# First batch in text order with a fence behind it, and weight maxima spread by TensorE, in a filter-and-experts kernel

## The chip, the cores and the metric

The kernel runs on one core of one Trainium2 chip. The metric is the device time of one execution in microseconds (us), the median over several runs. Engines are named as in the profile: PE is TensorE's matmul side (PEld its weight load), DVE is VectorE, ACT is ScalarE, POOL is GpSimd, SP is SyncE, which here only issues DMAs.

## What is computed

```python
def _attn_ref(x, filt_r, filt_i):            # x: 8 x 2496 x 256
    X = np.fft.rfft(x, axis=1)
    Y = X * (filt_r + 1j * filt_i)[None, :, :]
    return np.fft.irfft(Y, n=x.shape[1], axis=1)

def _moe_ref(x, expert_emb, tau, w1, w2):    # x: 19968 x 256, 8 experts, F = 1024
    xn = x / (norm(x) + 1e-06); en = expert_emb / (norm(expert_emb) + 1e-06)
    logits = xn @ en.T / tau
    expert_idx = np.argmax(logits, axis=1)
    gate_w = softmax(logits)[arange(N), expert_idx]
    for e in range(8):
        mask = expert_idx == e
        out[mask] = gate_w[mask, None] * (np.maximum(x[mask] @ w1[e], 0.0) @ w2[e])
```

A filter along the sequence, then each row goes to the expert with the largest cosine and comes back weighted.

## The kernel before

The eight batches go one after the other through four stages. **S1** (`conv_s1`): 11 tiles of x, each a product with the constant c1 (L403), a copy on ACT (L426) and a write to SD in DRAM. **S2** (`conv_s2`): ten tiles `a` read back from SD; product with c2, copies `xs` that swap the two halves on ACT (L486, L487), filter multiplications on DVE (`yy` L458, `xs` L460), the sum on POOL (L494; for batch 0 there is none, and the product with m1 is taken over both), product with m1 (L512), copy `z` (L515), write to ZD. **SB** (`conv_sb`, the tile loop): 11 tiles of ZD; product `y` (L403), squares on ACT (L587), a power of two near the norm on DVE (`q` L590, `rr` L592), the row's high half on ACT (L559) and low half on DVE (L562), transposes (L606), their copy `yT` on DVE (L608), logits `lp` (L621). A tile's high and low halves are taken one step later than its product and its transposes two. After every four tiles `route` (from L632) makes norms, the choice of an expert, the rank within it (L682) and indices (L704) in small DVE operations, and POOL scatters the rows to XS, grouped by expert (L711). **Slots**: 256 rows of one expert and batch, read transposed from XS (L834); `up` (product `ph` L865, high half `h` on ACT L871, low half on DVE L872), `down` (`po` L892) and a scatter to the output (L900). Slots of a batch run between the stages of the next one.

Weights arrive in fourteen DMAs of 1 MB issued by ACT (L210), each expert's in the place that the next expert's halves will take. `weight_halves` prepares them: largest absolute value along each partition (DVE, L242, L243), the largest over partitions (POOL's all-reduce, L246), scales (L249 to L257), then halves: ACT L271 or L267 and L268, DVE L272, POOL L269.

Most of the program is ordered by a scheduler. `head()` is the first batch: S1 of batch 0, its S2, its SB with batch 1's S1 woven in. In it the instructions of ACT and PE stand in text order (`manual_schedule`), those of the other engines where the scheduler puts them. Step numbers of `head()` set the weights: `WLOADS` gives the steps at which a load is issued (every fourth from the fourth), and from step 20 on preparation goes at 0.6 parts a step. No slot begins before `head()` has ended.

```python
    with tc.manual_schedule(engines={mybir.EngineType.Activation, mybir.EngineType.PE}):
        for n, _ in enumerate(head()):
            for _ in range(WLOADS.get(n, 0)):
                next(loads, None)
            if n >= PREP_AT:
                owed += PREP_RATE
```

Of the kernel before, what the change touches and what calls it, by code (L numbers as in the profile page):

```python
# [49 lines left out]
DLAG = 2  # L50
MID = 8
WLOADS = {4 + 4 * n: 1 for n in range(14)}
PREP_AT, PREP_RATE = 20, 0.6
# [3 lines left out]
def moe_spectral_kernel(  # L57
# [59 lines left out]
    emb_sb = cw.tile([E, D], F32, tag="hl", bufs=XYB, name="emb_sb")  # L117
    for t, a in ((c1_sb, c1), (c2_sb, c2), (m1_sb, m1), (csb_sb, csb), (sgn_sb, sgn),
                 (lt32, lt), (tau_sb, tau), (emb_sb, emb)):
        nc.scalar.dma_start(t, a)  # L120
# [5 lines left out]
    nc.vector.memset(one16, 1.0)  # L126

# [64 lines left out]


# [5 lines left out]
    wall = const.tile([P, E, 2], F32, tag="wall", name="wall")  # L199
# [35 lines left out]
    def weight_halves():  # L235
# [9 lines left out]
        def spread_max(e, js):  # L245
            nc.gpsimd.partition_all_reduce(wall[:, e, js], wmax[:, e, js], P, bass.bass_isa.ReduceOp.max)  # L246

        def scales(e, js):
            v.tensor_scalar(out=wall[:, e, js], in0=wall[:, e, js], scalar1=2.0 ** -100, scalar2=None, op0=ALU.max)  # L249
            v.tensor_scalar(out=wsc[:, e, js].bitcast(I32), in0=wall[:, e, js].bitcast(I32), scalar1=0x7F800000,  # L250
                            scalar2=0x7F800000, op0=ALU.bitwise_and, op1=ALU.bitwise_xor)
# [30 lines left out]
        for e in range(E - 1):  # L282
            if e + 1 < E - 1:
                yield from maxima(e + 1)
            scales(e, slice(0, 2))
            for j in range(4):
# [3 lines left out]
                yield  # L290
        e = E - 1
# [67 lines left out]
    def load(q, g, pool, tag, t, ap, rows, full):  # L359
        it = pool.tile([P, 2, D], F32, tag=tag, name=f"{tag}{g}_{t}")  # L360
        got = []
        for h, k, m in whole(g, ap, t, rows, full):
            q.dma_start(it[:k, h], m)  # L363
# [45 lines left out]

    def conv_s1(g):  # L410
# [20 lines left out]
    def conv_s2(g):  # L431
# [11 lines left out]
        def load_f(k):  # L443
            fts = []
            for k2 in range(k * 2 // nb, (k + 1) * 2 // nb):
                ft = cf.tile([P, 2, D], F32, tag="f", name=f"f{g}_{k2}")
                nc.sync.dma_start(ft, filt[k2])
                fts.append((k2, ft))
            return fts

# [12 lines left out]
        fin = {k: load_f(k) for k in range(2)}  # L463
# [4 lines left out]
        lag = SAL if g else 1  # L468
# [5 lines left out]
        for k in range(NK + lag):  # L474
            if k + INB - 1 < NK:
                ain[k + INB - 1] = load_a(k + INB - 1)
            if k < NK:
                pt = ps_c.tile([P, 2, D], F32, tag="c", name=f"s2_{g}_{k}")
# [13 lines left out]
                ys[k] = [yy]  # L492
# [5 lines left out]
                if k + 2 < NK:  # L498
                    fin[k + 2] = load_f(k + 2)
            yield W_S2  # L500
            j = k - 1
            if g >= G_SA and 0 <= j < NK:
                (_, a), = split(*asides(f"yp{g}_{j}"), [(both, ys[j][0].rearrange("p j c -> p (j c)"))])
                ys[j] = [a]
            j = k - lag
            if 0 <= j < NK:
                zp = ps_c.tile([P, CW], F32, tag="c", name=f"sa_{g}_{j}")
                for n, t in enumerate(ys[j]):
                    if isinstance(t, tuple):
                        product(zp, cons["m1"], t)  # L510
                    else:
                        nc.tensor.matmul(zp, cons["m1"], t.rearrange("p j c -> p (j c)"), start=(n == 0),  # L512
                                         stop=(n + 1 == len(ys[j])))
                zt = cst.tile([P, CW], F32, tag="st", name=f"z{g}_{j}")
# [4 lines left out]
    def conv_sb(g):  # L519
# [22 lines left out]
        if g == G_SB:  # L542
            cons["csb"] = parts_of(cons["csb"], "csb")
        for s in range(NTL + LPL):
            if s + 3 < NTL:
                vin[s + 3] = load_v(s + 3)
            if g >= G_SB:
                for u in (0, 1) if s == 0 else (s + 1,):
                    if u < NTL:
                        vin[u] = split(*pair(f"vp{g}_{u}"), vin[u])  # L550
            part()

            t = s - 1
            if 0 <= t < NTL:
# [5 lines left out]
                for i in range(2):  # L560
                    u = t % CHUNK * 2 + i
                    nc.vector.scalar_tensor_tensor(out=rows[:, i, D:2 * D], in0=y[:, i], scalar=rr[:, u:u + 1],  # L562
                                                   in1=rows[:, i, 0:D], op0=ALU.mult, op1=ALU.subtract)
            t = s
            if t < NTL:
                c = t // CHUNK
                if t % CHUNK == 0:
# [6 lines left out]
                        "rr": rt.tile([P, NTC], F32, tag="rr", name=f"rr{g}_{t}"),  # L574
                    }
# [9 lines left out]
                for i in range(2):  # L585
# [11 lines left out]
                               pattern=[[S if nb == 2 else TOK, 2]], base=b * S + ag * TOK, channel_multiplier=1)  # L597
            yield W_SB
# [33 lines left out]
    def route(g, out_rows, t0, n, rows, ssq, rr, lp):  # L632
# [15 lines left out]
        ssq, rr = ssq[:, :nt], rr[:, :nt]  # L648
# [456 lines left out]
```

## Time and profile before

| | |
|---|---|
| runs of before, us | 1512.34, 1515.03, 1509.94; median 1512.34 |
| profiled execution, us | 1499.08 (span 1497.2) |
| mean granted TensorE clock | 0.924 |
| busy share of the span | PE 87%, PEld 66%, DVE 58%, ACT 46%, POOL 37% |
| bytes moved by DMA | 229.16 MB, 153 GB/s in the mean |

The profiled execution was 13.3 us shorter than the median of the runs, so the working is made against its own 1499.08 us. Busy shares are means over the whole span; the first 219 us, before the first slot's hidden tile, look different from the rest, and are read by stretch. In the rows, idle time stands in square brackets with what ended it.

### The profile page before, as it was taken

The numbers are of one execution on the slowest core, as the hardware profiler recorded it, in microseconds if no ns is written. First come the engines' busy times: TensorE is split into PE (matmuls) and PEld (weight loads), VectorE is DVE, ScalarE is ACT, GpSimd is POOL, SyncE is SP. The second block draws the span as 40 slices with busy tenths as digits, with TensorE's granted clock in tenths as the row PEclk, the third lists the DMA queues.
The fourth block names the chain that finished last, engine by engine and source line by source line (L and its number), as shares of the span: only waits on it lengthen the run. The fifth ranks groups of instructions, "written<-read, shape, count | busy, mean of one in ns | idle before, by whom it ended". The sixth has DMA issues, their size and how long they took to land.

```text
span 1497.2 us, 31982 instructions
## 1 busy us (share of the span) xinstructions
PE 1301.8 (87%) x10956; PEld 988.2 (66%) x10956; DVE 873.5 (58%) x2841; ACT 693.7 (46%) x1578; POOL 548.7 (37%) x614
## 2 busy tenths in 40 slices
PE   5644557998997998899979988997999789999997
PEld 1212235766765776686658666865787578899997
DVE  2558765563474757575648555664658432266664
ACT  2435554543562665375437634662665122333332
POOL 0021454245524543552445254525433431222222
PEclk7876678999998999999989999999999889999999
DMA  8865375646774775577457746674753222122211
GB/s 273 302 213 200 118 211 158 187 133 189 215 188 130 205 217 156 166 220 183 140 166 201 195 121 185 195 192 124 200 169 92 76 67 54 50 49 48 49 45 40
DMA packets 230494, 229.16 MB, mean 153 GB/s; under 512 B 126089, under 2 KB 172497, under 8 KB 228405
## 3 DMA queue, kind: packets, MB, share of 16 engines
q1 hardware_dynamic: 200908, 151.93, 37.7%
q0 software_dynamic: 26400, 60.07, 12.8%
q10 hardware_dynamic: 3017, 15.02, 3.0%
q8 instruction: 92, 1.51, 0.4%
q14 instruction: 77, 0.63, 0.1%
HBM read 121.61 MB, written 84.84 MB: 138 GB/s over the span
## 4 chain that ended last, share of the span: by engine, by line
PE 61%; issue 15%; POOL 3%; DMA 2%; ACT 1%; DVE 1%; another core or an unknown queue 1%; POOLq 0%; SPq 0%; ACTq 0%; DVEq 0%
PE po L892 22%; PE ph L865 21%; PE y L403 5%; PE s L403 5%; POOL out_dram L900 3%; PE tp L606 2%; PE sa L408 2%; PE s L408 2%; DMA f<-ZD 1%; PE lp L621 1%; PE sa L512 1%; DMA ZD<-z 1%; DVE xs L460 0%; DMA f<-in_filt 0%
## 5 line engine op out<-in xcount | busy, mean ns | idle before, releaser
L892 PE MATMUL po<-W,h 128*128 128x256 f16 (+1 forms) x3864 | 519.8, 279 | 27.9 <-issue 27.5
L892 PEld LDWEIGHTS <-h 128*128 128x128 f16 x3864 | 375.5, 100 | 132.4 <-issue 85.3
L865 PE MATMUL ph<-xT,W 128*128 128x256 f16 x3072 | 414.8, 279 | 30.9 <-issue 18.7
L872 DVE SCALAR_TENSOR_TENSOR h<-ph,h 128x512 f16<-128x512 f32 (+1 forms) x388 | 232.0, 598 | 277.6 <-ACT h L871 240.6
L865 PEld LDWEIGHTS <-W 128*128 128x128 f16 x3072 | 300.1, 100 | 129.0 <-issue 91.4
L871 ACT ACTIVATE h<-ph 128x512 f16<-128x512 f32 (+1 forms) x388 | 203.4, 525 | 378.8 <-PE ph L865 205.4
L900 POOL DMA_INDIRECT out_dram<-o,meta x161 | 171.5, 1065 | 359.0 <-ACT o L899 319.4
L711 POOL DMA_INDIRECT XS<-rows,ixi x176 | 176.6, 1004 | 172.4 <-issue 136.2
L403 PE MATMUL y<-f,csb_sb 120*128 120x512 f32 (+1 forms) x192 | 101.2, 612 | 39.8 <-DVE rows L562 17.7
L494 POOL TENSOR_TENSOR yy<-yy,xs 128x512 f32<-128x512 f32 x70 | 94.3, 1349 | 109.1 <-DVE xs L460 69.5
L363 POOL DMA_DIRECT2D in<-in_x x84 | 66.9, 797 | 154.9 <-PE s L403 113.4
L403 PE MATMUL s<-in,c_sb 117*128 117x512 f32 (+1 forms) x192 | 111.1, 672 | 12.8 <-DMA in<-in_x 8.1
L865 PE MATMUL ph<-xT,wp 128*128 128x128 f16 x1584 | 104.9, 219 | 0.2
L865 PEld LDWEIGHTS <-wp 128*128 128x128 f16 x1584 | 96.7, 98 | 3.2 <-issue 0.7
L587 ACT ACTIVATE rows<-y 128x256 f16<-128x256 f32 x176 | 66.0, 384 | 64.7 <-PE y L403 58.8
L559 ACT ACTIVATE rows<-y,rr 128x256 f16<-128x256 f32 x176 | 73.9, 473 | 46.8 <-DVE rr L592 44.7
L426 ACT COPY s<-s 128x512 f32<-128x512 f32 x88 | 51.5, 586 | 91.4 <-PE s L403 43.5
L458 DVE TENSOR_TENSOR yy<-s,f 128x256 f32<-128x256 f32 x160 | 60.9, 419 | 52.5 <-ACT xs L487 39.4
L562 DVE SCALAR_TENSOR_TENSOR rows<-y,rr,rows 128x256 f16<-128x256 f32 x176 | 77.1, 478 | 22.5 <-ACT rows L559 19.8
L853 DVE COPY wp<-W 128x1024 f16 x132 | 62.1, 471 | 45.3 <-PE ph L865 44.8
L899 ACT ACTIVATE o<-po,meta 128x256 f32<-128x256 f32 x161 | 69.4, 475 | 34.2 <-PE po L892 26.7
L460 DVE SCALAR_TENSOR_TENSOR xs<-xs,sgn_sb,f 128x256 f32<-128x256 f32 x160 | 82.0, 551 | 0.0
(170 smaller groups left out, 1397.0 us busy)
## 6 DMA issues: line engine op xcount, KB each, us to landing
f<-in_filt SPq DMA_DIRECT2D x160, 256.0 KB
a<-SD SPq DMA_DIRECT2D x80, 256.0 KB
ZD<-z SPq DMA_DIRECT2D x80, 256.0 KB
SD<-s SPq DMA_DIRECT2D x80, 240.0 KB
f<-ZD SPq DMA_DIRECT2D x80, 240.0 KB
in<-in_x POOLq DMA_DIRECT2D x70, 234.0 KB
W<-in_w ACTq DMA_DIRECT2D x14, 1024.0 KB
XS<-rows,ixi POOLq DMA_INDIRECT x176
```

Source lines behind the costliest of these rows:

```text
L403: nc.tensor.matmul(out_, c[:a.shape[0]], a, start=True, stop=True)
L460: nc.vector.scalar_tensor_tensor(out=o, in0=i, scalar=sgn_sb[:, k2:k2 + 1], in1=f, op0=ALU.mult, op1=ALU.mult)
L494: nc.gpsimd.tensor_tensor(out=yy, in0=yy, in1=xs, op=ALU.add)
L559: nc.scalar.activation(rows[:, i, 0:D], y[:, i], AF.Copy, scale=rr[:, u:u + 1])
L562: nc.vector.scalar_tensor_tensor(out=rows[:, i, D:2 * D], in0=y[:, i], scalar=rr[:, u:u + 1], in1=rows[:, i, 0:D], op0=ALU.mult, op1=ALU.s ...
L711: i = nc.gpsimd.indirect_dma_start(out=XS, out_offset=bass.IndirectOffsetOnAxis(ap=ix, axis=0), in_=src, in_offset=None)
L865: last["pe"] = nc.tensor.matmul(ph[:, fi, :size], wp[:, k * 2 + wh, fi * P:(fi + 1) * P], xT[:, xh * 2 + k], start=(c == 0), stop=(c == 5))
L871: nc.scalar.activation(h[:, 0, :, :size], ph[:, :, :size], AF.Relu)
L872: hd = nc.vector.scalar_tensor_tensor(out=h[:, 1, :, :size], in0=ph[:, :, :size], scalar=0.0, in1=h[:, 0, :, :size], op0=ALU.max, op1=ALU. ...
L892: nc.tensor.matmul(self.po[:, s], self.hs[fp][:, hh, fi, s * P:(s + 1) * P], self.Wp[:, off + wh * 1024:off + wh * 1024 + D], start=(fp == ...
L899: nc.scalar.activation(o, self.po[:, s], AF.Copy, scale=self.meta[:, s, 1:2])
L900: i = nc.gpsimd.indirect_dma_start(out=out, out_offset=bass.IndirectOffsetOnAxis(ap=self.meta[:, s, 0:1].bitcast(I32), axis=0), in_=o, in_ ...
```

## The change

- DVE and SP stand in text order in `head()` too, and a fence of the scheduler (`no_sync_barrier`) behind it keeps later work from moving ahead of it.
- Constants: c1 and c2 on ACT's queue, the rest on POOL's. The experts' embeddings are prepared after S1 (`experts_ready`).
- Batch 0's x loads are all issued at once; all twenty filter slabs are loaded ahead (`FAHEAD`) into the places of experts 5 to 7 in W, four by SP and sixteen by ACT.
- Batch 0's S1 alternates between the two PSUM tiles of `ps_c` and the two of `ps_y`; its S2 has c2's products in `ps_y` and m1's in `ps_c`. It has the sum on POOL and one m1 product a tile, two steps later, as the other batches.
- In batch 0's SB a step first makes the new tile's product and squares, then the earlier tile's halves. Norms are taken out of `route` (`norms`), after the chunk's last squares.
- x loads of later batches are issued behind POOL's last sum.
- The maximum over partitions comes from two small products (one with an fp32 identity, one with ones) and five DVE operations.
- Weights: `WLOADS` names eight steps: expert 0's two loads in S2, those of experts 1 to 3 in SB; the other six behind the fence. `PREPS` prepares expert 0 alone in `head()`.

```diff
-WLOADS = {4 + 4 * n: 1 for n in range(14)}
-PREP_AT, PREP_RATE = 20, 0.6
+FAHEAD = 10
+WLOADS = (22, 26, 44, 50, 56, 62, 68, 72)
+PREPS = (35, 36, 40, 42, 44, 46)
...
         def spread_max(e, js):
-            nc.gpsimd.partition_all_reduce(wall[:, e, js], wmax[:, e, js], P, bass.bass_isa.ReduceOp.max)
+            n = js.stop - js.start
+            m = wmax[:, e, js]
+            v.tensor_scalar(out=m, in0=m, scalar1=2.0 ** -100, scalar2=None, op0=ALU.max)
+            v.tensor_scalar(out=m.bitcast(I32), in0=m.bitcast(I32), scalar1=0x7F800000, scalar2=None,
+                            op0=ALU.bitwise_and)
+            pm = ps_c.tile([P, 2, P], F32, tag="c", name=f"pm{e}_{js.start}")
+            nc.tensor.matmul(pm[:n, 0], m, ident32, start=True, stop=True)
+            v.tensor_reduce(out=wtop[:n, e:e + 1], in_=pm[:n, 0], axis=AX.X, op=ALU.max)
+            v.tensor_scalar(out=wdg[:n, e, :n], in0=ident32[:n, :n], scalar1=wtop[:n, e:e + 1], scalar2=None,
+                            op0=ALU.mult)
+            nc.tensor.matmul(pm[:, 1, :n], one32[:n], wdg[:n, e, :n], start=True, stop=True)
+            v.tensor_scalar(out=wsc[:, e, js].bitcast(I32), in0=pm[:, 1, :n].bitcast(I32), scalar1=0x7F800000,
+                            scalar2=None, op0=ALU.bitwise_xor)
...
+            (nc.scalar if not g and k > 1 else nc.sync).dma_start(ft, filt[k2])
...
+            alone = g == 0 and t % 2
+            pt = (ps_y if alone else ps_c).tile([P, 2, D], F32, tag="y" if alone else "c", name=f"s1_{g}_{t}")
...
+                pt = (ps_c if g else ps_y).tile([P, 2, D], F32, tag="c" if g else "y", name=f"s2_{g}_{k}")
...
-                if g:
-                    nc.gpsimd.tensor_tensor(out=yy, in0=yy, in1=xs, op=ALU.add)
-                else:
-
-                    ys[k].append(xs)
+                last["sum"] = nc.gpsimd.tensor_tensor(out=yy, in0=yy, in1=xs, op=ALU.add)
...
+            for stage in (quantised, rows_of) if g else (rows_of, quantised):
+                stage(s)
...
-    with tc.manual_schedule(engines={mybir.EngineType.Activation, mybir.EngineType.PE}):
+    engines = {mybir.EngineType.Activation, mybir.EngineType.PE, mybir.EngineType.DVE, mybir.EngineType.SP}
+    with tc.manual_schedule(engines=engines):
         for n, _ in enumerate(head()):
-            for _ in range(WLOADS.get(n, 0)):
+            if n in WLOADS:
                 next(loads, None)
-            if n >= PREP_AT:
-                owed += PREP_RATE
-            while owed >= 1:
-                owed -= 1
+            if n in PREPS:
                 next(prep, None)
+    tc.no_sync_barrier()
```

How this moves instructions is shown at three places. First ScalarE, from the last copies of batch 0's S1 to the first of its S2 (`s` is S1's copy, `xs` the swapped halves of S2, W the weights' place). Before:

```order
L426 COPY s0_7_290<-s1_0_7_288 128x512
L426 COPY s0_8_295<-s1_0_8_293 128x512
L210 DMA W_201<-in_w2 128x2048
L426 COPY s0_9_301<-s1_0_9_299 128x512
L426 COPY s0_10_307<-s1_0_10_304 128x512
L210 DMA W_201<-in_w1 128x2048
L486 COPY xs0_0_330<-s2_0_0_328 64x512
L487 COPY xs0_0_330<-s2_0_0_328 64x512
L486 COPY xs0_1_346<-s2_0_1_344 64x512
L487 COPY xs0_1_346<-s2_0_1_344 64x512
```

After:

```order
L472 COPY s0_8_268<-s1_0_8_266 128x512
L472 COPY s0_9_273<-s1_0_9_271 128x512
L472 COPY s0_10_279<-s1_0_10_276 128x512
L182 ACTIVATE esq_283,ess_284<-emb_sb_124 8x256
L190 CAST ehl_305<-esc_303 8x256
L447 DMA W_170<-in_filt 128x512 x16
L526 COPY xs0_0_344<-s2_0_0_342 64x512
L527 COPY xs0_0_344<-s2_0_0_342 64x512
L526 COPY xs0_1_357<-s2_0_1_355 64x512
L527 COPY xs0_1_357<-s2_0_1_355 64x512
```

The two weight loads are gone from here; the squares of the embeddings and sixteen loads of filter slabs stand ahead of the first `xs`.

Second VectorE in the middle of batch 0's tile loop (`rows` is the row buffer, `y` the inverse product, `q` and `rr` the power of two, `wmx` and `wmax` the weights' maxima, `wsc` their scale). Before:

```order
L242 TENSOR_REDUCE wmx_207<-W_201 128x1
L272 SCALAR_TENSOR_TENSOR W_201<-W_201,wsc_205 128x1024
L242 TENSOR_REDUCE wmx_207<-W_201 128x1
L562 SCALAR_TENSOR_TENSOR rows0_4_728<-y0_4_729,rr0_4_727,rows0_4_728 128x256 x2
L590 TENSOR_SCALAR q0_5_786<-ssq0_4_726 128x2
L272 SCALAR_TENSOR_TENSOR W_201<-W_201,wsc_205 128x1024
L243 TENSOR_REDUCE wmax_203<-wmx_207 128x1
L272 SCALAR_TENSOR_TENSOR W_201<-W_201,wsc_205 128x1024
L592 TENSOR_SCALAR rr0_4_727<-q0_5_786 128x2
L242 TENSOR_REDUCE wmx_207<-W_201 128x1 x2
L249 TENSOR_SCALAR wall_204<-wall_204 128x2
L608 COPY yT0_4_845<-tp0_4_836 128x1024
```

After:

```order
L655 COPY yT0_1_674<-tp0_1_665 128x1024
L621 TENSOR_SCALAR q0_4_695<-ssq0_4_687 128x2
L623 TENSOR_SCALAR rr0_4_688<-q0_4_695 128x2
L589 SCALAR_TENSOR_TENSOR rows0_3_627<-y0_3_628,rr0_0_539,rows0_3_627 128x256 x2
L655 COPY yT0_2_720<-tp0_2_711 128x1024
L621 TENSOR_SCALAR q0_5_737<-ssq0_4_687 128x2
L623 TENSOR_SCALAR rr0_4_688<-q0_5_737 128x2
L589 SCALAR_TENSOR_TENSOR rows0_4_690<-y0_4_691,rr0_4_688,rows0_4_690 128x256 x2
L655 COPY yT0_3_754<-tp0_3_745 128x1024
L621 TENSOR_SCALAR q0_6_778<-ssq0_4_687 128x2
L623 TENSOR_SCALAR rr0_4_688<-q0_6_778 128x2
L589 SCALAR_TENSOR_TENSOR rows0_5_732<-y0_5_733,rr0_4_688,rows0_5_732 128x256 x2
```

The reductions and halves of weights are gone from between a tile's operations, which now follow one another tile by tile.

Third VectorE up to the first hidden tile `h` of the first slot. Before:

```order
L242 TENSOR_REDUCE wmx_207<-W_201 128x1 x2
L458 TENSOR_TENSOR yy1_3_1577<-s2_1_3_1572,f1_6_1506 128x256
L458 TENSOR_TENSOR yy1_3_1577<-s2_1_3_1572,f1_7_1508 128x256
L460 SCALAR_TENSOR_TENSOR xs1_3_1574<-xs1_3_1574,sgn_sb_121,f1_6_1506 128x256
L243 TENSOR_REDUCE wmax_203<-wmx_207 128x1
L460 SCALAR_TENSOR_TENSOR xs1_3_1574<-xs1_3_1574,sgn_sb_121,f1_7_1508 128x256
L242 TENSOR_REDUCE wmx_207<-wraw0_1621 128x1
L242 TENSOR_REDUCE wmx_207<-wraw1_1623 128x1
L249 TENSOR_SCALAR wall_204<-wall_204 128x1
L872 SCALAR_TENSOR_TENSOR h0_0_0_1414<-ph0_0_0_1401,h0_0_0_1414 128x512
```

After:

```order
L252 TENSOR_REDUCE wmax_172<-wmx_177 128x1
L272 TENSOR_SCALAR wsc_175<-wsc_175 128x1 x2
L251 TENSOR_REDUCE wmx_177<-W_170 128x1 x2
L274 RECIPROCAL winv_176<-wsc_175 128x2
L291 SCALAR_TENSOR_TENSOR W_170<-W_170,wsc_175 128x1024
L252 TENSOR_REDUCE wmax_172<-wmx_177 128x1
L276 TENSOR_TENSOR isc_171<-winv_176 128x1
L291 SCALAR_TENSOR_TENSOR W_170<-W_170,wsc_175 128x1024
L258 TENSOR_SCALAR wmax_172<-wmax_172 128x2
L251 TENSOR_REDUCE wmx_177<-W_170 128x1 x2
L291 SCALAR_TENSOR_TENSOR W_170<-W_170,wsc_175 128x1024
L923 SCALAR_TENSOR_TENSOR h0_0_0_1275<-ph0_0_0_1262,h0_0_0_1275 128x512
```

Between the last index of batch 0 (L755) and this first `h` (L923) there stand, after the change, 22 of the reductions L251, nine of the halves L291 (experts 1 to 3), 11 of L252, some 44 small operations, and one tile of batch 1's filter; before, most of the weights' operations stood ahead of the last index, and parts of four filter tiles of batch 1 behind it.

## Rows read from the trace of the kernel before

**Rows 1.** Chain that ended last, shares by line (page).
```profile
PE po L892 22%; PE ph L865 21%; PE y L403 5%; PE s L403 5%; POOL out_dram L900 3%; PE tp L606 2%; PE sa L408 2%; PE s L408 2%; DMA f<-ZD 1%; PE lp L621 1%; PE sa L512 1%; DMA ZD<-z 1%; DVE xs L460 0%; DMA f<-in_filt 0%
```

**Rows 2.** By stretch: length, busy PE, PEld, DVE, ACT, POOL, granted clock, DMA share, GB/s.
```profile
4.00:29.00 25.00, 18.81 (x28) 6.37 (x28) 6.14 (x25) 7.73 (x15) 0.00 (x0) 0.80 0.93 288
40.50:93.50 53.00, 35.42 (x60) 12.43 (x60) 33.67 (x70) 22.66 (x35) 7.06 (x7) 0.83 0.81 281
101.80:164.80 63.00, 32.18 (x166) 15.94 (x166) 47.56 (x142) 34.78 (x82) 14.72 (x23) 0.69 0.58 187
164.80:188.80 24.00, 13.75 (x85) 7.92 (x86) 19.67 (x95) 13.37 (x22) 14.80 (x15) 0.57 0.39 116
188.80:219.40 30.60, 13.75 (x41) 6.00 (x40) 18.92 (x33) 13.94 (x19) 19.95 (x17) 0.68 0.77 212
260.00:400.00 140.00, 132.89 (x1043) 96.69 (x1042) 74.08 (x282) 67.45 (x163) 62.27 (x72) 0.98 0.62 181
```

**Rows 3.** TensorE's timeline: start us, us, line, tiles, count, idle before and releaser.
```profile
40.53 3.75 PE L403 MATMUL s<-a,c_sb 128*128 128x512 f32 x4 [11.61 <-DMA a<-SD]
...
101.80 2.08 PE L403 MATMUL y<-f,csb_sb 120*128 120x512 f32 x2 [8.96 <-DMA f<-ZD]
...
126.93 1.13 PE L403 MATMUL y<-f,csb_sb 120*128 120x512 f32 x2
...
137.71 2.08 PE L403 MATMUL y<-f,csb_sb 120*128 120x512 f32 x2 [7.22 <-DVE rows L562]
...
164.76 2.37 PE L403 MATMUL y<-f,csb_sb 120*128 120x256 f32 x4 [6.35 <-DVE rows L562]
...
212.95 2.78 PE L865 MATMUL ph<-xT,W 128*128 128x256 f16 x24 [0.76 <-DMA xT<-XS]
...
219.53 1.47 PE L865 MATMUL ph<-xT,W 128*128 128x256 f16 x12 [1.97 <-DVE wsc L250]
...
241.01 1.44 PE L865 MATMUL ph<-xT,W 128*128 128x256 f16 x6 [4.35 <-DVE wsc L253]
```

**Rows 4.** VectorE's timeline, same columns.
```profile
45.52 0.76 DVE L458 TENSOR_TENSOR yy<-s,f 128x256 f32<-128x256 f32 x2 [0.16 <-ACT xs L487]
46.20 0.87 DVE L460 SCALAR_TENSOR_TENSOR xs<-xs,sgn_sb,f 128x256 f32<-128x256 f32 x2
...
188.37 0.45 DVE L704 CAST ixi<-ix 128x1 int32<-128x1 f32 x6
...
218.72 0.15 DVE L249 TENSOR_SCALAR wall<-wall 128x1 f32<-128x1 f32 x1 [3.89 <-POOL wall L246]
218.79 0.68 DVE L872 SCALAR_TENSOR_TENSOR h<-ph,h 128x512 f16<-128x512 f32 x1
```

**Rows 5.** ScalarE's timeline: last copy of S2, a DMA issue.
```profile
92.89 0.58 ACT L515 COPY z<-sa 128x512 f32<-128x512 f32 x1 [8.35 <-PE sa L512]
92.89 0.34 ACTq L210 DMA_DIRECT2D W<-in_w  x1
```

**Rows 6.** By stretch, VectorE's L242 (weight reductions) alone.
```profile
40.50:93.50 53.00, 11.71 (x10) 0.83 0.81 281
101.80:164.80 63.00, 11.84 (x10) 0.69 0.58 187
```

**Rows 7.** Groups by line and shape, 0 to 260 us: GpSimd.
```profile
L494 POOL TENSOR_TENSOR yy<-yy,xs 128x512 f32<-128x512 f32 x9 | 11.7, 1303 | 15.6 <-DMA ZD<-z 7.9 <-ACT h L871 7.3 <-DVE xs L460 0.5
...
L246 POOL PARTITION_ALL_REDUCE wall<-wmax x9 | 3.3, 369 | 101.5 <-DVE wmax L243 56.8 <-issue 27.6 <-DVE rr L592 10.1
```

**Rows 8.** By stretch, VectorE's L272 (weight halves) alone.
```profile
101.80:164.80 63.00, 10.20 (x8) 0.69 0.58 187
```

**Rows 9.** Groups by line and shape, 0 to 260 us: tile loop.
```profile
L562 DVE SCALAR_TENSOR_TENSOR rows<-y,rr,rows 128x256 f16<-128x256 f32 x22 | 9.6, 477 | 4.2 <-ACT rows L559 4.0
...
L559 ACT ACTIVATE rows<-y,rr 128x256 f16<-128x256 f32 x22 | 9.2, 472 | 24.5 <-DVE rr L592 24.5
...
L587 ACT ACTIVATE rows<-y 128x256 f16<-128x256 f32 x22 | 8.3, 387 | 13.0 <-PE y L403 12.9
```

More of the change, by code (lines that the diff above doesn't have):

```diff
@@ L290, in weight_halves @@
                 yield
+            if e == 0:
+                yield from maxima(1)
         e = E - 1
@@ L359, in load @@
     def load(q, g, pool, tag, t, ap, rows, full):
-        it = pool.tile([P, 2, D], F32, tag=tag, name=f"{tag}{g}_{t}")
+        if pool is rowp:
+            it = pool.tile([P, 2, ROW], F16, tag="rows", name=f"{tag}{g}_{t}").rearrange("p j c -> p (j c)")
+            it = it.bitcast(F32)[:, :2 * D].rearrange("p (j c) -> p j c", j=2)
+        else:
+            it = pool.tile([P, 2, D], F32, tag=tag, name=f"{tag}{g}_{t}")
         got = []
         for h, k, m in whole(g, ap, t, rows, full):
-            q.dma_start(it[:k, h], m)
+            with behind("sum") if q is nc.gpsimd else ExitStack():
+                q.dma_start(it[:k, h], m)
             got.append((h, it[:k, h].rearrange("p j c -> p (j c)")))
@@ L408, in product, with load_f @@
             nc.tensor.matmul(out_, w[:k], b, start=(n == 0), stop=(n == 2))
+    fin0 = {}
+    def load_f(g, k):
+        nb = GROUPS[g]
+        fts = []
+        for k2 in range(k * 2 // nb, (k + 1) * 2 // nb):
+            if g:
+                ft = cf.tile([P, 2, D], F32, tag="f", name=f"f{g}_{k2}")
+            else:
+                ft = W32[:, E - 3:].rearrange("p e c -> p (e c)")[:, k2 * CW:(k2 + 1) * CW]
+                ft = ft.rearrange("p (r c) -> p r c", r=2)
+            (nc.scalar if not g and k > 1 else nc.sync).dma_start(ft, filt[k2])
+            fts.append((k2, ft))
+        return fts
     def conv_s1(g):
@@ L461, in filtered @@
                                                    op1=ALU.mult)
-        fin = {k: load_f(k) for k in range(2)}
+        fin = {k: load_f(g, k) for k in range(2)} if g else fin0
+        ahead = 2 if g else FAHEAD
+        for k in range(2, ahead):
+            fin[k] = load_f(g, k)
         yield W_GAP
@@ L473, in conv_s2 @@
         both = slice(0, 2)
-        for k in range(NK + lag):
+        for k in range(NK + SAL):
             if k + INB - 1 < NK:
@@ L540, in part, with quantised @@
                 out_rows.pop(0)()
[L542 to L551, printed above, removed]
+        def quantised(s):
             t = s - 1
@@ L574, in conv_sb @@
                         "rr": rt.tile([P, NTC], F32, tag="rr", name=f"rr{g}_{t}"),
+                        "f": rt.tile([P, NTC], F32, tag="fn", name=f"fn{g}_{t}"),
                     }
@@ L630, in conv_sb, with norms, route @@
             yield from zero_rows(state["base"])
-    def route(g, out_rows, t0, n, rows, ssq, rr, lp):
+    def norms(g, t0, n, ssq, rr, f):
+        sg, n0 = (rt1.tile([P, NTC], F32, tag=k, name=f"{k}{g}_{t0}")[:, :n] for k in ("sg", "n0"))
+        norm_eps(sg, ssq[:, :n], n0)
+        nc.vector.scalar_tensor_tensor(out=f[:, :n], in0=sg, scalar=tau64, in1=rr[:, :n], op0=ALU.mult, op1=ALU.mult)
+        nc.vector.reciprocal(f[:, :n], f[:, :n])
+        yield 1
+    def route(g, out_rows, t0, n, rows, ssq, rr, lp, f):
         tg = f"{g}_{t0}"
@@ L928, in later @@
             yield -1
-    loads, prep, owed = weight_loads(), weight_halves(), 0.0
+    loads, prep = weight_loads(), weight_halves()
     def head():
         yield from conv_s1(0)
+        experts_ready()
         yield from conv_s2(0)
```

129 lines of the change are left out of this document (68 added, 61 removed).

## Prediction

> **What bounds the kernel now.** I read the chain of waits first: TensorE carries 61% of it, and the two products of the slots, `po` and `ph`, lead it [rows 1]. So an edit pays where TensorE is not yet kept busy. The table of engine time by stretch says where that is [rows 2]. Between 260 and 400 us TensorE is busy 132.9 of 140 us; ahead of 219.4 us it never comes near that: 32 of 63 us in the tile loop of the first batch (101.8 to 164.8), 14 of 24 in the tail that ends with its indices, 14 of 31 from there to the first hidden tile `h`. That is a head of 219 us in which the first batch goes through alone, and what is cut from it moves everything behind it forward, since behind it TensorE is the bound. Third I read TensorE's timeline for the points that divide the head [rows 3]: first inverse product at 40.5 after 11.6 us of waiting for `a`, which comes back from DRAM; first `y` at 101.8; last `y` at 164.8, 6.35 us late because of `rows` on VectorE; first `ph` at 213.0. The first `h` is at 218.8 [rows 4].
>
> **The change by those points**, before and after. All 'after' times are estimates from the rows named.
>
> A. *First copy of S2, 42.6 → 32.* Up to there SD and `a` must come round through DRAM (first product at 40.5, 2.1 us long). S1 moves 2.56 MB of x, 2.62 MB of SD and 1.05 MB of filter, 6.2 MB; at the 288 GB/s of the first stretch [rows 2] 21.6 us, plus 3 to start (chosen), 24.5. That S2 started at 42.6 is partly owed to weight loads of 1 MB that ScalarE issues in S1 (order, first place), which the change takes away. It adds sixteen filter slabs there, ahead of the first copy. Issuing one takes 0.34 us [rows 5], sixteen 5.4. In the built program each waits for the one eight places ahead, so about half of 4.2 MB must land first: 7.3 us at that rate. I take 32. Ends: 27 (issue time alone) and 42 (no gain).
>
> Here a page speaks against the change. The Trainium skill, page "DMA: Bandwidth & Descriptors", section "Issuing engines are not separate DMA queues", says that a second issuing engine saves only issue time, since all share the same sixteen engines. By it the point stays near 42, which is a rival below.
>
> B. *S2, 42.6 to first `y` at 101.8 → 32 to 65.* Before, ten tiles took 51 us (42.6 to 93.5), with ten weight reductions among VectorE's work, 11.7 us [rows 6]; `z` waited 8.35 us at the end [rows 5]. After, no weight work stands on VectorE here, the filters are loaded, and a tile has two products instead of three. A tile is then bounded below by VectorE's filter, 0.76 + 0.87 = 1.6 us [rows 4], and above by two products at the lower clock, 2 × 2.08 = 4.2 (the product of `y` has the same size and took 1.13 at the higher clock) [rows 3]. I take 2.1, nearer to the lower end because the granted clock was 0.83 in this stretch [rows 2], most of the way to the full one: 21 us, and 4 for the first copies (1.2), the new sum on GpSimd (1.30, [rows 7]), the last product and its copy. S2 ends at 57. `z` to `y` through DRAM took 8.3 us (copy at 92.9, 0.6 long, `y` at 101.8) and has no reason to change: 65. Ends for S2: 20 and 46 us. Expert 0's maxima and spread stand under this round trip; without that cover they would cost 6 us.
>
> C. *Tile loop, 63 us → 50.* A tile took 6.3 us. TensorE's own work in it was 32.2 us, 3.2 a tile, at a clock of 0.69 [rows 2]: the lower end. The upper end is 6.3. VectorE had 47.6 us of work there, of which ten reductions and eight halves made 22 [rows 6, 8]; the change takes these out of the text order (order, second place), which leaves 2.5 a tile, and it removes the 7.2 and 6.35 us in which TensorE waited for `rows` [rows 3]. I take 5.0: those two waits with a little of the smaller ones, 13 of 63 us. I do not take 3.2, because with two PSUM tiles for `y` a chain still runs through the engines: product (1.1 to 2.1), two squares (0.39 each), two high halves (0.47), two low halves (0.48) [rows 3, 9] make 3.8 to 4.8. Last `y`: 115.
>
> D. *Tail, 24.0 → 23.* The same chain of routing operations and scatters; the norms go a little ahead. Indices: 138.
>
> E. *Indices to first `h`, 30.0 → 48.* This is where the change takes something back. Before, most weight work was done in the head. The order of VectorE (third place) shows that between the last index and the first `h` now stand 22 reductions (22 × 1.18 = 26.0), nine halves (9 × 1.28 = 11.5) [rows 6, 8], 11 combining reductions and some 44 small operations (0.15 each, [rows 4]: 8.3) and one filter tile of batch 1 (1.6): 47.4, and 0.7 for `h`. So "the first expert's weights alone ahead of slots" holds for the head only: e1 to e3 are halved, and e4, e5 and half of e6 reduced, before the first `h`. First `h`: 186, gain 33. Low end: 24 us, which the scatters and the transposed load take before the first `ph` (188.8 to 213.0); high end 62, if the six loads issued behind the fence, 6.3 MB with some 5 MB of other traffic, move at the 212 GB/s of that stretch [rows 2], 54 us, and four reductions with their small operations, some 8, follow the last.
>
> F. *The maxima by TensorE, 6 gained.* The all-reduce itself takes 0.37 us, but GpSimd idles 27.6 us round nine of them with nothing that the profile shows it waiting for, and more behind them [rows 7]; VectorE waits 3.89 us for one [rows 4], and TensorE 1.97 and 4.35 behind the scales that follow it [rows 3]. Two products and five small operations (0.15) take its place, about 1.5 us of latency. The 3.89 lies ahead of the first `h` and is in E already; behind it TensorE's two waits make 6.3, and the 1.5 us lie beside other work of VectorE, so I take 6, with 0 and 10 as ends.
>
> The Trainium skill, page "VectorE: DVE Perf Modes", section "Why `tensor_reduce` can't reduce along partition axis", sends such reductions to GpSimd. By it term F would be zero or a loss of 1; the row of 3.89 us speaks against it here.
>
> G. *Weight halves of e4 to e7 among the slots, −5.* Four experts' halves that were partly done before now share VectorE with `h`; VectorE was busy 74 of 140 us [rows 2], which hides most. Ends 0 and −16.
>
> **Sum**: 33 + 6 − 5 = 34 us. From the profiled execution's 1499.1 us (span 1497.2) that gives 1465. The median of the runs shown is 13.3 us above that execution, so on its scale 1512.3 − 34 = **1478**.
>
> **Rivals.**
> - *Everything frees up.* Tile loop 4.0 a tile (its chain's middle) and S2 at 27: another 15 us, **1463**. For: the clock rises when TensorE waits less (0.69 against 0.98, [rows 2]). 0.13.
> - *ScalarE is held by the sixteen filter loads.* S2's copies stand behind them in text order and start at 42 as before: 10 us back, **1488**. For: x, SD and slabs share the transfer rate, 93% busy in that stretch [rows 2]. 0.14.
> - *Loads behind the fence land late.* The last loads needed for the reductions ahead of the first `h` come at the 62 us end: 15 lost, **1493**. 0.10.
> - *The shift is eaten among the slots.* Halves and maxima of e4 to e7 stop TensorE there as the scales did at 219 and 241 [rows 3], several times over: **1510**, no change. Against: only two such stops were seen before. 0.06.
> - *Slower: text order makes the tile loop one serial chain.* VectorE, ScalarE and TensorE all in text order, each tile's steps waiting for the other engines' at the lower clock: y 2.08, squares 0.8, high halves 0.9, low halves 0.9, transposes 1.1, their copy 0.7, logits 0.5, batch 1's product 1.9, VectorE's routing share 2: 10.8 us a tile, 58 over the forecast, **1536**. It decides from 8.4 us a tile on (5.0 + 34/10). For: TensorE waited 7.2 us for `rows` already [rows 3]; against: those waits stood behind reductions that go. 0.06.
>
> **How the numbers follow.** Forecast 0.51, the rivals 0.13, 0.14, 0.10, 0.06, 0.06. A measurement of this kernel tells 0.3%, 4.5 us, from no change. Faster by more: 0.51 + 0.13 + 0.14 + 0.10 = 0.88; within: 0.06; slower: 0.06. The range goes from the first rival with some of the low ends (1455) to the late loads with the long end of G (1507); beyond lie about 2 in 10.
>
> **What would show it.** Right: S2's first copy near 32, ten tiles under 26 us, first `y` near 65, last near 115, first `h` near 186, no GpSimd stop with an all-reduce, VectorE full between the indices and `h`. Wrong: a first copy at 42 behind ScalarE's loads; tiles over 8 us; TensorE idle behind `L251` or `L291` after 230 us.

## The result, and the profile after

The change made the kernel **slower: 1525.1 us** median (1517.5 to 1528.6) against 1507.7 for the kernel before, ratio 1.0108, 95% interval 1.0086 to 1.013. The forecast was 1478. The profiled execution of after has a span of 1520.6 us.

The head, the first batch alone, gained nearly what was forecast. These are its points in the trace of after: engine time by stretch (columns as in [rows 2]),

```profile
28.00:41.00 13.00, 3.75 (x4) 1.12 (x4) 0.88 (x3) 2.03 (x4) 0.00 (x0) 0.50 1.03 373
41.00:69.00 28.00, 20.64 (x36) 7.17 (x36) 19.38 (x42) 15.31 (x27) 14.77 (x13) 0.87 0.64 220
77.00:124.40 47.40, 32.02 (x165) 15.87 (x166) 30.49 (x111) 24.02 (x71) 11.79 (x21) 0.75 0.74 206
124.40:147.00 22.60, 13.01 (x85) 7.28 (x83) 14.10 (x72) 5.04 (x14) 10.04 (x11) 0.50 0.68 201
147.00:190.00 43.00, 12.15 (x43) 6.32 (x44) 42.86 (x93) 20.05 (x23) 17.00 (x15) 0.58 0.76 271
```

TensorE's timeline, with the first `y` of the batches that answer to [rows 3],

```profile
28.53 3.75 PE L429 MATMUL s<-a,c_sb 128*128 128x512 f32 x4 [1.68 <-DMA a<-SD]
41.13 2.05 PE L429 MATMUL s<-a,c_sb 128*128 128x512 f32 x2 [8.85 <-DMA W<-in_filt]
...
76.83 2.04 PE L429 MATMUL y<-f,csb_sb 120*128 120x512 f32 x2 [4.02 <-DMA f<-ZD]
...
124.44 2.21 PE L429 MATMUL y<-f,csb_sb 120*128 120x256 f32 x4
...
176.51 4.63 PE L916 MATMUL ph<-xT,W 128*128 128x256 f16 x24 [1.70 <-DMA xT<-XS]
...
404.21 1.12 PE L429 MATMUL y<-f,csb_sb 120*128 120x512 f32 x2 [3.21 <-DMA f<-ZD]
...
556.36 2.07 PE L429 MATMUL y<-f,csb_sb 120*128 120x512 f32 x2 [7.33 <-DMA f<-ZD]
...
849.56 2.08 PE L429 MATMUL y<-f,csb_sb 120*128 120x512 f32 x2 [3.38 <-DMA f<-ZD]
```

and VectorE's timeline at the first hidden tile.

```profile
187.73 1.85 DVE L291 SCALAR_TENSOR_TENSOR W<-W,wsc 128x1024 f16<-128x1024 f32 x1
189.50 0.68 DVE L923 SCALAR_TENSOR_TENSOR h<-ph,h 128x512 f16<-128x512 f32 x1
```

First `y` at 76.8 (101.8 in [rows 3]), last `y` at 124.4 (164.8), first `h` at 189.5 (218.8 in [rows 4]): 29 us gained. From 147 to 190 us, between the last indices and that `h`, VectorE is busy 42.9 of 43 us. So the loss lies behind the head. There TensorE waits at the first `y` of five later batches for `f` from ZD, up to 7.33 us. The list of waits, 250 to 1300 us, has it in one line (us in total, times, longest): after,

```profile
PE y L429 <- DMA f<-ZD: 19.1, 5, 7.3
```

and before.

```profile
PE y L403 <- DMA f<-ZD: 2.4, 4, 1.4
```

What comes in the way of the round trip through ZD is put there by GpSimd's order. Its timeline in after, ahead of the 7.33 us wait,

```profile
531.32 1.28 POOL L533 TENSOR_TENSOR yy<-yy,xs 128x512 f32<-128x512 f32 x1 [3.59 <-DVE xs L498]
536.18 1.26 POOL L533 TENSOR_TENSOR yy<-yy,xs 128x512 f32<-128x512 f32 x1 [3.59 <-DVE xs L498]
537.39 3.23 POOL L389 DMA_DIRECT2D in<-in_x  x4
```

beside the same place of before:

```profile
525.50 1.26 POOL L494 TENSOR_TENSOR yy<-yy,xs 128x512 f32<-128x512 f32 x1
526.95 1.04 POOL L900 DMA_INDIRECT out_dram<-o,meta  x1 [0.19 <-DMA f<-in_filt]
527.97 0.85 POOL L363 DMA_DIRECT2D in<-in_x  x1
528.84 1.81 POOL L494 TENSOR_TENSOR yy<-yy,xs 128x512 f32<-128x512 f32 x1
530.60 0.81 POOL L363 DMA_DIRECT2D in<-in_x  x1
```

Before, the x loads of the next batch stand one by one between the sums of S2. After, four of 234 KB are issued together behind the last sum, because `behind("sum")` holds for every batch; the trace has such four in each of the six batches whose successor's x is loaded this way. They then move at the same time as the last `z` to ZD. The chain of after shows the price:

```profile
540.52 0.59 ACT z L551
541.11 0.02 issue
541.13 11.57 DMA ZD<-z
...
552.77 3.54 DMA f<-ZD
```

In before, SyncE's timeline shows 2.5 us from the last `z` of that batch to the first load of `f` behind it; here 11.6 us pass.

```profile
546.08 0.32 SPq L516 DMA_DIRECT2D ZD<-z  x1
...
548.53 0.83 SPq L363 DMA_DIRECT2D f<-ZD  x2
```

The DMA share of that stretch (last but one number) says the same: after,

```profile
541.00:553.00 12.00, 7.29 (x52) 5.12 (x51) 1.73 (x3) 2.47 (x5) 4.00 (x7) 0.97 1.08 167
```

and before.

```profile
546.00:549.00 3.00, 3.00 (x24) 2.21 (x22) 0.89 (x2) 1.65 (x4) 0.49 (x1) 1.00 0.63 174
```

The sixteen DMA engines are full in after and were not in before.

### The profile page after: what moved, and what is told of

Read it like the earlier page. It is cut to its first block, busy times and chain, and to the rows that moved or that the text cites. A ratio compares the mean times of both kernels' runs of the same rounds, so it can differ in the third digit from the quotient of the medians.

```text
span 1520.6 us, 32052 instructions
## 1 busy us (share of the span) xinstructions
PE 1308.6 (86%) x10972; PEld 992.5 (65%) x10972; DVE 876.8 (58%) x2870; ACT 693.6 (46%) x1578; POOL 555.2 (37%) x621
## 4 chain that ended last, share of the span: by engine, by line
PE 57%; issue 16%; DMA 9%; DVE 7%; POOL 4%; ACT 4%; another core or an unknown queue 2%; SPq 1%; POOLq 0%; ACTq 0%; DVEq 0%
PE ph L916 19%; PE po L943 18%; PE y L429 6%; PE s L429 5%; POOL out_dram L951 3%; PE tp L653 2%; DMA ZD<-z 2%; PE s L434 2%; PE sa L434 2%; DMA f<-ZD 2%; DMA a<-SD 1%; PE sa L429 1%; DVE wmx L251 1%; PE lp L668 1%
## 5 line engine op out<-in xcount | busy, mean ns | idle before, releaser
L916 PE MATMUL ph<-xT,W 128*128 128x256 f16 x3072 | 417.0, 281 | 21.1 <-issue 11.3
L923 DVE SCALAR_TENSOR_TENSOR h<-ph,h 128x512 f16<-128x512 f32 (+1 forms) x388 | 231.6, 597 | 278.0 <-ACT h L922 223.4
L916 PEld LDWEIGHTS <-W 128*128 128x128 f16 x3072 | 304.3, 101 | 116.3 <-issue 75.0
L533 POOL TENSOR_TENSOR yy<-yy,xs 128x512 f32<-128x512 f32 x80 | 106.9, 1337 | 216.2 <-DVE xs L498 128.4
L429 PE MATMUL y<-f,csb_sb 120*128 120x512 f32 (+1 forms) x192 | 105.2, 635 | 32.7 <-DMA f<-ZD 23.1
L429 PE MATMUL s<-in,c_sb 117*128 117x512 f32 (+1 forms) x192 | 106.0, 648 | 10.6 <-DMA in<-in_x 5.9
L586 ACT ACTIVATE rows<-y,rr 128x256 f16<-128x256 f32 x176 | 73.5, 475 | 31.5 <-DVE rr L623 23.9
L496 DVE TENSOR_TENSOR yy<-s,f 128x256 f32<-128x256 f32 x140 | 52.9, 418 | 51.5 <-ACT xs L527 34.8
L653 PEld LDWEIGHTS <-rows 128*128 128x128 f16 x704 | 50.3, 101 | 37.3 <-issue 33.7
```

The lines of the kernel that those rows point to most:

```text
L429: nc.tensor.matmul(out_, c[:a.shape[0]], a, start=True, stop=True)
L533: last["sum"] = nc.gpsimd.tensor_tensor(out=yy, in0=yy, in1=xs, op=ALU.add)
L586: nc.scalar.activation(rows[:, i, 0:D], y[:, i], AF.Copy, scale=rr[:, u:u + 1])
L653: nc.tensor.transpose(tp[:, i, j], rows[:, i, j * P:(j + 1) * P], ident)
L916: last["pe"] = nc.tensor.matmul(ph[:, fi, :size], wp[:, k * 2 + wh, fi * P:(fi + 1) * P], xT[:, xh * 2 + k], start=(c == 0), stop=(c == 5))
L923: hd = nc.vector.scalar_tensor_tensor(out=h[:, 1, :, :size], in0=ph[:, :, :size], scalar=0.0, in1=h[:, 0, :, :size], op0=ALU.max, op1=ALU. ...
```

## The experiments

The kernels ran in five groups, each on one chip and beside the kernel before. Ratios are to it, with their 95% interval; its medians were 1507.7 us beside the change, 1498.3 (e1 to e4), 1406.9 (e5, e6, e8, e9), 1507.8 (f1 to f3, e7) and 1508.7 (g1 to g4). Letters stand for theories, which the expectations state where they first come up: H is the held x loads, P the late weights, N the norms.

**x loads.** e1 takes the order away, e3 keeps it for batch 1, e2 puts it into the kernel before.

```diff
-            with behind("sum") if q is nc.gpsimd else ExitStack():
+            with behind("sum") if g == 1 and q is nc.gpsimd else ExitStack():
```

> The changed kernel, with the x loads of all batches free of the order behind GpSimd's last sum; nothing else changed. Theory H (held x loads): in the changed kernel four x loads stand behind the last sum of every S2 and meet the round trip of z through ZD, which costs 3 to 10 us in each of seven batches; free, the time falls by 30 to 50 us from 1525, to 1475 to 1495, and the first y of the batches come every 137 to 145 us as before. Theory P (preparation of experts 4 to 7 among the slots eats the head's gain): the loss lies in the first two batches, and the time stays within 8 us of the changed kernel's. Theory N (norms as a part of their own lengthen the tile loop's steps): no change either, below 5 us.

> The kernel before with one edit: x loads of later batches stand behind the last sum on GpSimd, as in the change. Theory H: slower by 20 to 45 us than before, with TensorE waiting for f from ZD at the start of most tile loops. Theories P and N: within 5 us of before, since weights and norms are as before.

> The changed kernel with the x loads held behind the last sum for batch 1 alone. Theory H: within 3 us of the kernel with all x loads free, since batch 1's loads stand in the same place in both. Theories P and N: within 8 us of the changed kernel.

e2: 1529.8 us, ratio **1.0218** (1.0187 to 1.0249); its waits show `PE y L404 <- DMA f<-ZD: 19.5, 6, 5.0`. That one order makes the kernel before 31.5 us slower. e3: 1491.6, ratio 0.9971 (0.9939 to 1.0002). e1 has no ratio: its four runs took 1489, 1484, 4461 and 3268 us, and why is not known; its order behind batch 1 is that of e3, and its profiled span was 1487.6 against 1488.9. H stands: the held loads cost time when they are put into one kernel, and give it back when they are taken out of the other. Its 30 to 50 us for e1 were too many (21.1 us below). That P and N had said no change refutes them only as the sole cause; what they name is tried next.

**Norms.** e4 is the change with the norms inside the routing again; e5 is e3 with that edit too.

```diff
-                if t % CHUNK * 2 + 2 == ck["n"]:
-                    parts.append(norms(g, ck["t0"], ck["n"], ssq, rr, ck["f"]))
...
+        for _ in norms(g, t0, n, ssq, rr, f):
+            pass
```

> The changed kernel with the norms computed inside the routing again, x loads held as in the change. Theory N: faster by 10 to 30 us, most of it as shorter tile loops of batches 1 to 7 (35 to 39 us each in the changed kernel, 32 to 35 before). Theory H: within 5 us of the changed kernel, perhaps 3 slower since the first batch's tail has its norms back.

> The changed kernel with two edits undone behind the head: x loads held behind the last sum for batch 1 alone, and the norms inside the routing again. Theory H+N (both cost time in every later batch): below the kernel with the first edit alone, 7 us under before in its pair: by 4 to 12 us more, so a ratio to before of 0.987 to 0.994. Theory H alone: ratio 0.994 to 1.000, as with the first edit alone.

e4: ratio 1.0079 (1.0051 to 1.0108), where the change had 1.0108 on another chip; N's 10 to 30 us are not there. e5: 1385.0 us on a chip where before took 1406.9, ratio 0.9845 (0.9796 to 0.9894). To part the two edits, f1 (the change), f2 (e3) and f3 (e5) ran on one chip.

> The changed kernel itself, so that it, the edit on the x loads, and the edit on x loads and norms are timed on one chip. Slower than before, ratio 1.005 to 1.03.

> The changed kernel with x loads held for batch 1 alone, on the same chip. Theory H: 15 to 30 us faster than the changed kernel of this call, ratio to before 0.985 to 1.000.

> The same with the norms inside the routing. Theory H+N: a further 4 to 15 us faster, ratio to before 0.978 to 0.992, and most of it as shorter distances between the first y of later batches. Theory H alone: within 3 us of the run with the first edit alone.

f1: 1525.3, ratio 1.0108 (1.0062 to 1.0153). f2: 1504.2, ratio 0.997 (0.9936 to 1.0003). f3: **1497.8, ratio 0.9926** (0.9896 to 0.9957). By these medians the x loads cost 21.1 us and the norms 6.4. The intervals of f2 and f3 overlap, but their single times, ten and nine on one chip, differ by 7.1 us in the mean, with an interval of 2.8 to 11.4 worked out from them; so the norms cost something too. Why is not shown: in the table of first `y` below f3 gains it in one step, from batch 4 to 5 (139.9 us against f2's 147.0), not in every batch. f3 beats both kernels.

**The all-reduce put back** (on e5).

```diff
-            pm = ps_c.tile([P, 2, P], F32, tag="c", name=f"pm{e}_{js.start}")
...
+            nc.gpsimd.partition_all_reduce(wall[:, e, js], wmax[:, e, js], P, bass.bass_isa.ReduceOp.max)
...
```

> The kernel of the run with both edits undone, with GpSimd's all-reduce in place of the two products and their small operations. If the all-reduce stops VectorE and GpSimd as in the kernel before (3 to 5 us each, some of it covered): 4 to 12 us slower than that kernel. If the spread is worth nothing: within 3 us.

1421.6 us, ratio 1.0096 (1.0059 to 1.0133) where e5 has 0.9845: 36.6 us slower, three times the most that was expected. In its trace the first all-reduce behind the indices stands behind the scatters (the last began at 155.68), GpSimd idles 8.36 us ahead of it for nothing that the profile shows, and TensorE waits behind VectorE, its first `yy` standing behind the weights: the timelines of GpSimd, VectorE and TensorE.

```profile
165.09 0.37 POOL L255 PARTITION_ALL_REDUCE wall<-wmax  x1 [8.36 <-issue]
```

```profile
165.49 0.17 DVE L258 TENSOR_SCALAR wall<-wall 128x2 f32<-128x2 f32 x1 [8.86 <-POOL wall L255]
```

```profile
188.30 2.04 PE L419 MATMUL s<-a,c_sb 128*128 128x512 f32 x2 [24.48 <-DVE yy L486]
```

The first `h` comes at 204.9 against e5's 180.8, so 24 of the 36.6 us are lost by there.

**Slot supply.** e8 and g4 lay batch 1's stages faster over batch 0's slots.

```diff
-            run["pace"] = steps / (4 * len(queue) - MARGIN)
+            run["pace"] = steps / (4 * len(queue) - (7 if run["g"] == 0 else MARGIN))
```

> The kernel with both edits undone, with the stages of batch 1 laid faster over the eight slots of batch 0 (25 units in place of 29), so that about one slot is left when batch 1's routing ends. Theory S (the head's gain is lost at the end of batch 1's tile loop, since batch 0's slots run out before batch 1's rows are scattered; TensorE idle 7 us and more there): that stop shrinks, the second and third batch's first y come 5 to 12 us earlier, time 4 to 10 us less. Rival (the gain is lost to the weights' halves among the slots): within 3 us or slower.

> The changed kernel with both edits undone and batch 1's stages laid faster over batch 0's slots, on this chip. Theory S: 3 to 8 us faster than without that (ratio to before near 0.989). Rival: within 3 us, as on the chip of the first trial.

e8: 1385.9 beside e5's 1385.0. g4: ratio 0.9916 (0.9886 to 0.9946) beside f3's 0.9926 on another chip. Batch 1's first `y` came 9.4 us earlier in e8 (240.8 against 250.2), and the time did not follow: the edit is worth nothing. Theory S itself stays open, since the stop that it names did not shrink. It shows as TensorE's wait for the first sum of batch 2's S2, in the waits of f3 from batch 1's first `y` to batch 2's,

```profile
PE sa L429 <- POOL yy L533: 4.5, 1, 4.5
```

and in those of g4, where a stop behind a late weight half comes on top.

```profile
PE sa L429 <- POOL yy L533: 8.9, 1, 8.9
PE po L942 <- ACT W L290: 7.6, 1, 7.6
```

**Maxima behind the first h** (on e5).

```diff
-                v.tensor_reduce(out=wmx[:, i:i + 1], in_=r, axis=AX.X, op=ALU.max, apply_absolute_value=True)
+                with behind("h") if e >= 3 else ExitStack():
+                    v.tensor_reduce(out=wmx[:, i:i + 1], in_=r, axis=AX.X, op=ALU.max, apply_absolute_value=True)
...
+            last.setdefault("h", hd)
```

> The kernel with both edits undone, with the weight maxima of experts 3 to 7 ordered behind the first hidden tile on VectorE: 8 reductions and one half stand ahead of it in place of 20 and 6. If VectorE's block sets the first h (43 us between the last index and it, VectorE busy 42.9 of them): first h 10 to 20 us earlier, and if that carries to the end, 8 to 18 us less; if weights then stop the slots of experts 1 to 4, as much is given back as TensorE's waits for wsc and W show, and the time is within 4 us. By theory S the first h comes earlier and the end does not, unless batch 1's S2 moves with it.

1398.4, ratio 0.9943 (0.9913 to 0.9972): 13.4 us slower than e5. The first `h` moved only from 180.8 to 175.3 (10 to 20 us expected), since TensorE now waits 11.9 us for `xT` ahead of it, and batch 1's first `y` moved from 250.2 to 267.0. The work was put where it costs more.

**Filter slabs issued by GpSimd** (on f3).

```diff
-            (nc.scalar if not g and k > 1 else nc.sync).dma_start(ft, filt[k2])
+            (nc.gpsimd if not g and k > 1 else nc.sync).dma_start(ft, filt[k2])
```

> The last kernel with batch 0's sixteen ahead-loaded filter slabs issued by GpSimd in place of ScalarE. If ScalarE is held by its own sixteen issues (12.8 us between the S1 copies and the first copy of S2 in the changed kernel): the first copy comes at 31 to 34 us in place of 38.9, first y 4 to 8 us earlier, and 3 to 8 us less in all if it carries to the end. If the sixteen DMA engines are the limit (full at 370 GB/s in that stretch): the first copy moves but the later tiles wait for a or for filters, and first y is within 2 us.

1505.6, ratio 0.9983 (0.9957 to 1.0009): 7.7 us slower than f3. GpSimd issued the slabs from 5.5 to 20.9 us, beside x and SD, and S1's last product moved from 19.5 (f3) to 31.8. TensorE's timeline of e7:

```profile
31.75 2.37 PE L429 MATMUL s<-in,c_sb 117*128 117x256 f32 x4 [4.31 <-ACT s L472]
...
40.61 3.75 PE L429 MATMUL s<-a,c_sb 128*128 128x512 f32 x4 [1.15 <-DMA a<-SD]
```

The first copy of S2 came at 42.7 in place of 39.3, the first `y` at 80.0 in place of 77.7. By stretch, f3

```profile
4.00:41.00 37.00, 17.91 (x32) 6.67 (x32) 4.76 (x33) 8.98 (x17) 1.73 (x8) 0.72 0.93 304
```

and e7

```profile
4.00:41.00 37.00, 17.43 (x29) 6.06 (x30) 4.42 (x31) 7.25 (x14) 10.41 (x24) 0.70 0.95 296
```

move nearly the same bytes a second, with the DMA engines nearly full (0.93 and 0.95). So their rate is the limit in this stretch, whoever issues. The Trainium skill, page "DMA: Bandwidth & Descriptors", section "Issuing engines are not separate DMA queues", says that DMAs run on the same sixteen engines whichever engine started them. This run agrees. But e7 also moved the slabs some 20 us forward, in among S1's transfers; slabs issued by another engine behind S1 were not tried.

**Late weights, and the fence.** On one chip: g1 the kernel before, g2 f3 with little of the late weights' work, g3 f3 without `tc.no_sync_barrier()`. In g2 the maxima and halves of experts 4 to 7 are taken of 64 columns only, and the slots of these experts, with the tail blocks, use the weights of experts 0 to 3.

```diff
+                r = r[:, :64] if e >= 4 else r
...
+                if e >= 4:
+                    raw, hi, lo = raw[:, :64], hi[:, :64], lo[:, :64]
...
-                self.Wp, self.isc = W[:, e], isc[:, e:e + 1]
+                self.Wp, self.isc = W[:, e % 4], isc[:, e % 4:e % 4 + 1]
...
```

> The kernel before, for its trace on the chip of this call: the first y of its batches there, beside which those of the other three are read. Span within 1 % of the runs of before.

> The changed kernel with x loads held for batch 1 alone and norms in the routing, in which maxima and halves of experts 4 to 7 work on 64 columns only and slots of these experts use the weights of experts 0 to 3 (tail blocks those of 0 to 3): it leaves out most of the late weights' preparation. Theory P (that preparation, moved from the head to among the slots, takes back part of the gain): 8 to 20 us faster than with it, most of it before the third batch's first y. Rivals: within 4 us.

> The changed kernel with both edits undone and without the scheduler's fence behind the head, so that later work may stand between the first batch's operations. Theory F (the fence is what makes the preparation of experts 1 to 3 stand in one block between indices and first h): without it the block is spread into the tail, first h 5 to 15 us earlier, time 3 to 12 us less. Rival: the tail's operations wait behind weights again, last index 5 to 10 us later, time within 4 us or more.

g2: 1476.4, ratio **0.978** (0.9737 to 0.9824), where f3 has 0.9926 on another chip: about 22 us (P: 8 to 20), an upper bound for the preparation, since in g2 slots also never wait for a late weight. g3: 1519.6, ratio 1.0083 (1.0055 to 1.0111), where f3 has 0.9926: 21 us slower by the medians, 24 by the ratios. Its tile loop took from 91.8 to 154.0 us, 62 as in before, with eight reductions and three halves of weights in it again, where f3 has none there, and its first `h` came at 223.4 (f3: 182.4). So without the fence the tile loop is not shorter; theory F falls, and its rival holds.

The first `y` of each batch in the traces, in us, shows where each loss stands:

| | batch 0 | 1 | 2 | 3 | 4 | 5 | 6 | 7 | span |
|---|---|---|---|---|---|---|---|---|---|
| g1 before | 102.6 | 274.2 | 413.2 | 555.7 | 694.5 | 837.1 | 981.9 | 1128.9 | 1507.4 |
| f1 change | 74.3 | 249.6 | 401.6 | 552.9 | 699.0 | 849.5 | 1005.5 | 1150.6 | 1522.5 |
| f2 x free | 74.3 | 248.4 | 398.8 | 544.1 | 685.1 | 832.1 | 979.6 | 1128.2 | 1502.8 |
| f3 and norms | 77.7 | 251.9 | 399.7 | 546.5 | 685.7 | 825.6 | 973.0 | 1119.3 | 1496.0 |
| g2 and late weights | 75.5 | 244.5 | 380.4 | 524.4 | 664.4 | 807.4 | 955.8 | 1101.5 | 1478.7 |

From batch 1 to batch 6 f1 loses 7 to 13 us on g1 in every step, 48 in all. f3's lead over g1 falls from 22.3 to 9.2 between batches 1 and 3 and then stays; g2's stays near 30 to the end. VectorE's groups of f3, 190 to 560 us, show what is there,

```profile
L291 DVE SCALAR_TENSOR_TENSOR W<-W,wsc 128x1024 f16<-128x1024 f32 x11 | 13.7, 1279 | 5.1 <-ACT W L290 5.0
...
L251 DVE TENSOR_REDUCE wmx<-W 128x1 f32<-128x1024 f32 x5 | 6.0, 1211 | 4.6 <-DMA W<-in_w 4.6
```

against g1, 190 to 560 us:

```profile
L272 DVE SCALAR_TENSOR_TENSOR W<-W,wsc 128x1024 f16<-128x1024 f32 x6 | 7.6, 1284 | 6.8 <-ACT W L271 6.8
...
L242 DVE TENSOR_REDUCE wmx<-W 128x1 f32<-128x1024 f32 x3 | 3.6, 1216 | 6.8 <-DMA W<-in_w 6.8
```

How this work costs time is not shown. From 222 to 1300 us no wait of a TensorE product in after, f1, f2 or f3 has a weight operation as its releaser. What the stretch from batch 1's first `y` to batch 2's does show, in which f3 loses 8.8 us on g1, is more work on VectorE, more idle time of TensorE (19 us against 9) and a lower clock: f3, g1 and g2.

```profile
251.90:399.70 147.80, 128.52 (x910) 85.97 (x908) 83.41 (x303) 69.97 (x164) 64.79 (x74) 0.90 0.66 178
```

```profile
274.20:413.20 139.00, 130.20 (x1019) 94.70 (x1019) 72.71 (x281) 66.54 (x161) 61.91 (x71) 0.98 0.64 178
```

```profile
244.50:380.40 135.90, 126.60 (x981) 89.64 (x979) 75.10 (x303) 65.93 (x164) 61.30 (x73) 0.97 0.70 194
```

## Why the prediction was wrong, point by point

- **A.** The first copy of S2 came at 38.9, forecast 32, end 42. The mechanism of the second rival was there: ScalarE's row reads

```profile
25.75 13.07 ACTq L447 DMA_DIRECT2D W<-in_filt  x16
38.92 0.58 ACT L526 COPY xs<-s 64x512 f32<-64x512 f32 x1 [12.79 <-DMA W<-in_filt]
```

 The held time is 13.1 us, not 7.3; e7, with another issuer, came later still.
- **B, C, D.** S2 to first `y` 37.9 us (forecast 33), tile loop 47.6 (50), tail 23.4 (23): right in kind and near in size. The slower rival (one serial chain, 10.8 us a tile) is refuted: a tile took 4.8. Text order alone did not make it so; without the fence it was 6.2 (g3).
- **E.** Indices to first `h` 41.6 (forecast 48), with VectorE full as said. Gain at `h`: 29, forecast 33. That this came out so near is partly luck: the first `y` was 11.8 us later than forecast, and the way from it to `h` 8.3 us shorter.
- **F.** Forecast 6; against the old order it was not measured by itself. In the new order the spread is worth 36.6 (e6 against e5): the all-reduce now stands behind 22 scatters, and batch 1's filter behind it. The Trainium skill, page "VectorE: DVE Perf Modes", section "Why `tensor_reduce` can't reduce along partition axis", sends reductions over partitions to GpSimd. Here the measurement decides against it.
- **G.** Mis-sized: forecast −5, with −16 as its end; g2 measured up to −22. The cover that I named, VectorE's 66 free us of 140, did not hide it: the late weights fall into the batches in which the head's lead has to be kept. By what wait they cost it stays open, as said above.
- **The step that failed** is the sentence that "what is cut from it moves everything behind it forward", with no term for what the change does to the order of the later batches (F and G are weights alone). The x loads' order behind the sum stood in the list of changes and was costed at nothing; GpSimd's order shows it in six batches, and it cost 21.1 us (f1 against f2). The norms, moved for all batches, cost about 6.
- **The sum.** Against before, by medians, g2 is 32.3 us faster, f3 10.0 faster, f2 3.6 faster and f1 17.4 slower; so the late weights take back 22.3, the norms 6.4 and the x loads 21.1. This closes by construction and checks nothing; g2 and f3 ran on different chips, so the 22.3 is approximate. Between the forecast of 34 gained and 17 lost lie 51 us. The x loads and the norms, which the sum did not have, make 27.5 of them, G up to 17, the head 4; the 3 that are left would be F's.

The rival "the shift is eaten among the slots" was the nearest: right that the gain is lost behind the head, and 15 us short. Its mechanism, halves and maxima that stop TensorE, is not what the traces of the change show, and it had no x loads and no norms. For the same reason the sign "TensorE idle behind `L251` or `L291` after 230 us" did not come, though the forecast was wrong.

## What to carry to other kernels

An ordering edge that is written for one stage and sits in a helper holds in every stage: compare each queue's order in a steady batch too, and ask which round trip a delayed burst of loads will meet. A gain in a head is only worth what the first steady stages can keep; work moved out of it has to be costed where it lands. A fence that costs nothing in work can be the part that pays.

## What was not expected of the hardware

The same kernel, e5 and f3, took 1385.0 us on one chip and 1497.8 on another, and the kernel before 1406.9 and 1507.8. In the list of waits TensorE's stops for nothing that the profile shows ("issue") make 75.1 us in f3's trace and 6.1 in e5's. In these traces it goes with the chip, not the kernel: 6 to 13 us in e5, e6, e8 and e9, which ran there, and 62 to 80 in all other traces. f3's largest:

```profile
PE po L942 <- issue: 40.5, 54, 3.8
PE ph L915 <- issue: 11.9, 20, 1.2
```

What causes them was not tried. The ratios to before differ with it (0.9845 and 0.9926), so a gain measured on one chip is not the gain on every one.
